# An attention and two feed-forward layers in one kernel: the scores of k in two parts, and the loads of v among those of k

## The chip, the cores and the metric

The kernel runs on one core of one Trainium2 chip. The metric is the device time of one execution in microseconds; the median of three runs is given.

## The reference, cut to what matters

All arrays are float32 at the kernel's inputs except the four weight matrices, which arrive as float64 bits and are converted on the chip. There are 12480 tokens of 128 channels and 49 agents.

```python
def sm(a, b):
    s = scale * (a @ b.transpose(0, 2, 1))
    s = s - s.max(-1, keepdims=True)
    e = np.exp(s)
    return e / (e.sum(-1, keepdims=True) + 1e-09)
agent_v = sm(agents, k) @ v            # 49 x 128, over all 12480 tokens
x = sm(q, agents) @ agent_v            # 12480 x 128
h = x @ w_in                           # 128 -> 2048
x = (h / (1 + np.exp(-h))) @ w_out     # 2048 -> 128
h = x @ w2_in
P = a[0] + a[1] * h + a[2] * h**2 + a[3] * h**3
Q = 1.0 + np.abs(b[0]) * np.abs(h) + np.abs(b[1]) * h**2
out = (P / (Q + 1e-6)) @ w2_out
```

The first softmax runs over all tokens of k, so agent_v needs the whole of k and of v, and every output token needs agent_v.

## The kernel before, in words

The tokens are cut into 25 groups of 512 (the last has 192), and two groups make a block of 1024 tokens (13 blocks, the last of 192 tokens). Every step has a short name, and one function emits its instructions.

**The start.** The loads are issued on SyncE's queue in the order of the string LOADS: a letter k or v is the next block of k or of v (512 KB, the last 96 KB), q is the first block of q, and any other character is one of 16 chunks of the weights (its code less 48: chunks 0 to 3 are w_in, 4 to 7 w_out, 8 to 11 w2_in, 12 to 15 w2_out; 512 KB each). The blocks of k and v go round a ring of 11 buffers, the weight chunks round a ring of 4; a load that finds its buffer in use waits at the head of the queue, and all later loads behind it. For a block b of k, KT transposes it on TensorE, KC copies it out of PSUM on ScalarE, KS makes the scores of the agents, KV keeps them in SBUF and KM (VectorE) takes their maximum. X0 to X2 join the 13 maxima and make the bias; then for each block EX takes exp with its sum on ScalarE, ET transposes on TensorE, EC copies on VectorE, and AV adds eT times v into one PSUM tile. F0 and F1 sum up, F2 divides, F3 and F4 turn the result into agent_v transposed (avT). A weight chunk is converted by C0 (VectorE, three passes), C1 (ScalarE, two), C2 (VectorE, two, the last to read the raw buffer) and C3 (GpSimd); the chunks of w2_in are also split into a high and a low part by C4 (ScalarE, w2h) and C5 (GpSimd, w2l). V0 to V2 multiply w_in by agent_v, which makes the weights w1a and w1b. q's softmax runs a block at a time in the steps QT to QBl.

**The main loop.** For a group g and each p of 8 pairs of 128 hidden channels: M1 (TensorE, h = xt by w1a and w1b), S1 (ScalarE, Silu), M2 (TensorE, into the PSUM tile x2). XS splits x2 into xh and xl. Then M3 (TensorE, three products, w2l and w2h), U, W1 and W2 make P without its last term, AB, N and Q (ScalarE, GpSimd, GpSimd) make the denominator, and L and R (ScalarE, Ln and Sigmoid with a change of table before each batch of four) its reciprocal; G2 joins them and M4 (TensorE) adds into the PSUM tile ot. O1 to O3 write out. M3 of group 0 needs all chunks of w2_in, and AB and U of group 0 need all 16 chunks converted.

**The order.** A planner in the kernel's own code, `scheduled`, writes out the order of all steps at build time: `group_steps` gives each step its engine, an assumed cost, what it comes after, which buffers it takes and ends the use of, and a place; of the steps that are ready on an engine within SLACK, the one with the lowest place goes first. The places are the table PLACE (one number for a step, or one for each p), with `<` and `>` added in the first two and last two groups. READY_Y is the number of halves of y that must be done in a group before its batch of L may begin. PSUM holds three tiles of two banks for h (slots 0 to 2), one bank called x2 and one called ot. On each engine the instructions run in the order written out.

## Time and profile before

| what | before |
|---|---|
| median of 3 runs | 1268.18 us (1267.84 to 1269.21) |
| the profiled execution's own time | 1269.22 us |
| its span, first to last instruction | 1267.4 us |
| TensorE (PE) busy | 1238.8 us, 98% of the span |
| ScalarE (ACT) busy | 1076.2 us, 85% |
| VectorE (DVE) busy | 1002.5 us, 79% |
| GpSimd (POOL) busy | 765.2 us, 60% |

Shares are means over the whole span, and the start, the main loop and the end have different limits. A busy PE is not PE at its peak, as matmuls are pipelined and run at the clock that is granted (1.00 is the full 2.4 GHz, 0.50 is 1.2 GHz). A wait is put down to the releaser that came last.

### The profile page before, as it was taken

To read this page: it belongs to the slowest core of one execution; us is meant where nothing else is said; L and a number is where in the kernel's file an instruction comes from. 1 tells how busy PE (TensorE), PEld (TensorE's weight loads), DVE (VectorE), ACT (ScalarE), POOL (GpSimd) and SP (SyncE) were. 2 spreads that over 40 slices of the span, in tenths; PEclk is the share of its full clock that TensorE was granted. 3 is DMA by queue.
4 is the path that set the end of the run, shared out by engine and by line. 5 is a ranking of instruction groups with operands and counts; after the bars stand their busy time and mean duration, and the time that the engine had idled before them with its cause. 6 is when DMAs were issued, how large, how long until landed. Compare 5 with 4: busy or idle time off the path is not lost.

```text
span 1267.4 us, 12079 instructions
## 1 busy us (share of the span) xinstructions
PE 1238.8 (98%) x4393; PEld 742.1 (59%) x4393; DVE 1002.5 (79%) x960; ACT 1076.2 (85%) x997; POOL 765.2 (60%) x434
## 2 busy tenths in 40 slices
PE   9899899999999999999999999999999999999987
PEld 5656555555556566566566565565555555555654
DVE  4977787878869869869869769769769769768894
ACT  7676888988988988988978978978978978978895
POOL 2247767567656656655755755755755755756873
PEclk9899899999999999999999999999999999999999
DMA  9820000000000000000000000000000000000000
GB/s 336 302 83 1 1 17 9 9 17 9 9 17 9 9 18 9 9 17 9 9 17 9 9 17 9 9 17 9 2 24 8 1 12 9 1 9 8 9 1 20
DMA packets 14675, 34.75 MB, mean 27 GB/s; under 512 B 1575, under 2 KB 5720, under 8 KB 14616
## 3 DMA queue, kind: packets, MB, share of 16 engines
q1 hardware_dynamic: 14616, 33.98, 7.5%
q8 instruction: 35, 0.57, 0.2%
q14 instruction: 24, 0.20, 0.1%
HBM read 27.59 MB, written 6.39 MB: 27 GB/s over the span
## 4 chain that ended last, share of the span: by engine, by line
PE 86%; DVE 6%; ACT 4%; DMA 3%; issue 1%; POOL 0%; SPq 0%; POOLq 0%; ACTq 0%; DVEq 0%
PE x L551 25%; PE ot L635 24%; PE h L537 7%; PE h L574 7%; PE h L538 7%; PE h L576 7%; PE h L575 7%; DVE z L610 2%; DVE z L614 1%; PE h L468 1%; DVE z L585 1%; PE h L451 1%; DMA kv<-in_k_dram 1%; DMA q<-in_q_dram 1%; PE ot L655 1%
## 5 line engine op out<-in xcount | busy, mean ns | idle before, releaser
L598 POOL TENSOR_SCALAR y<-m,bab 128x1024 f32<-128x1024 f32 (+1 forms) x200 | 266.0, 1333 | 410.0 <-ACT m L592 403.1
L606 POOL TENSOR_TENSOR y<-y,m 128x1024 f32<-128x1024 f32 (+1 forms) x200 | 469.1, 2357 | 7.5
L635 PE MATMUL ot<-z,w2o 128*128 128x512 f32 (+1 forms) x800 | 357.4, 587 | 7.5 <-DVE z L626 4.6
L551 PE MATMUL x<-s,wo 128*128 128x512 f32 (+1 forms) x800 | 357.6, 582 | 3.4 <-ACT s L544 3.2
L610 DVE TENSOR_TENSOR z<-z,h 128x1024 f32<-128x1024 f32 (+1 forms) x200 | 237.7, 1191 | 143.7 <-ACT z L583 136.6
L626 DVE SCALAR_TENSOR_TENSOR z<-z,a_sb,y 128x1024 f32<-128x1024 f32 (+1 forms) x200 | 263.0, 1365 | 4.7 <-ACT y L622 4.7
L592 ACT ACTIVATE m<-h 128x1024 f32<-128x1024 f32 (+1 forms) x200 | 197.1, 1000 | 81.1 <-PE h L576 72.7
L614 DVE SCALAR_TENSOR_TENSOR z<-z,a_sb,h 128x1024 f32<-128x1024 f32 (+1 forms) x200 | 249.9, 1251 | 5.0 <-ACT m L592 0.5
L635 PEld LDWEIGHTS ot<-z,w2o 128*128 128x128 f32 x800 | 149.1, 190 | 164.2 <-issue 146.1
L544 ACT ACTIVATE s<-h 128x1024 f32<-128x1024 f32 (+1 forms) x200 | 193.4, 1005 | 59.6 <-PE h L538 58.5
L551 PEld LDWEIGHTS x<-s,wo 128*128 128x128 f32 x800 | 147.3, 190 | 138.8 <-issue 126.9
L574 PE MATMUL h<-xh,w2l 128*128 128x512 f32 (+1 forms) x400 | 190.8, 477 | 1.7 <-DVE z L614 1.2
L619 ACT ACTIVATE y<-y,eps 128x2048 f32<-128x2048 f32 (+1 forms) x100 | 191.4, 1956 | 0.8 <-POOL y L606 0.5
L537 PE MATMUL h<-xt,w1a 128*128 128x512 f32 (+1 forms) x400 | 185.8, 466 | 0.7 <-DVE z L614 0.7
L622 ACT ACTIVATE y<-y 128x2048 f32<-128x2048 f32 (+1 forms) x100 | 184.9, 1878 | 0.3
L576 PE MATMUL h<-xh,w2h 128*128 128x512 f32 (+1 forms) x400 | 155.7, 389 | 0.0
L538 PE MATMUL h<-xt,w1b 128*128 128x512 f32 (+1 forms) x400 | 155.2, 389 | 0.0
L575 PE MATMUL h<-xl,w2h 128*128 128x512 f32 (+1 forms) x400 | 155.0, 387 | 0.0
L585 DVE TENSOR_SCALAR z<-h,a_sb 128x1024 f32<-128x1024 f32 (+1 forms) x100 | 130.9, 1313 | 5.7 <-PE h L576 3.8
L583 ACT ACTIVATE z<-h,a_sb 128x1024 f32<-128x1024 f32 (+1 forms) x100 | 118.3, 1184 | 8.3 <-PE h L576 4.6
L537 PEld LDWEIGHTS h<-xt,w1a 128*128 128x128 f32 x400 | 75.5, 189 | 43.6 <-issue 15.8
L574 PEld LDWEIGHTS h<-xh,w2l 128*128 128x128 f32 x400 | 75.7, 189 | 36.8 <-issue 20.6
(105 smaller groups left out, 849.5 us busy)
## 6 DMA issues: line engine op xcount, KB each, us to landing
q<-in_q_dram SPq DMA_DIRECT2D x12, 512.0 KB, 3.3
out_dram<-ob SPq DMA_DIRECT2D x24, 256.0 KB, 2.0
raw<-in_moe_w_in_dram SPq DMA_DIRECT2D x8, 512.0 KB, 5.4
raw<-in_moe_w_out_dram SPq DMA_DIRECT2D x8, 512.0 KB, 7.5
s<-in_k_dram SPq DMA_DIRECT2D x7, 512.0 KB, 8.4
kv<-in_v_dram SPq DMA_DIRECT2D x7, 512.0 KB, 7.4
kv<-in_k_dram SPq DMA_DIRECT2D x5, 512.0 KB, 10.2
s<-in_v_dram SPq DMA_DIRECT2D x5, 512.0 KB, 8.6
```

What stands on the lines that cost most here:

```text
L537: nc.tensor.matmul(h[:, c, :w], w1a[:, f], xt, start=True, stop=False)
L538: nc.tensor.matmul(h[:, c, :w], w1b[:, f], xt, start=False, stop=True)
L551: nc.tensor.matmul(x2_t[i][:, : cols(i)], wo[:, 2 * p + c, :], s[:, c, : cols(i)], start=(p == 0 and c == 0), stop=(p == NP - 1 and c == 1),)
L574: nc.tensor.matmul(h[:, c, :w], w2l[:, f], xh_t[i], start=True, stop=False)
L575: nc.tensor.matmul(h[:, c, :w], w2h[:, f], xl_t[i], start=False, stop=False)
L576: nc.tensor.matmul(h[:, c, :w], w2h[:, f], xh_t[i], start=False, stop=True)
L598: nc.gpsimd.tensor_scalar(out=y_t[i, p // 2][:, p % 2], in0=m_t[i, p], scalar1=bab[:, 1:2], scalar2=bab[:, 0:1], op0=ALU.mult, op1=ALU.add,)
L606: eng.tensor_mul(out=y, in0=y, in1=m_t.pop((i, p)))
L610: nc.vector.tensor_mul(out=z, in0=z, in1=h)
L614: nc.vector.scalar_tensor_tensor(out=z, in0=z, scalar=a_sb[:, 1:2], in1=h, op0=ALU.add, op1=ALU.mult)
L626: nc.vector.scalar_tensor_tensor(out=z, in0=z, scalar=a_sb[:, 0:1], in1=r, op0=ALU.add, op1=ALU.mult)
L635: nc.tensor.matmul(ot_t[i][:, : cols(i)], w2o[:, 2 * p + c, :], z[:, c, :], start=(p == 0 and c == 0), stop=(p == NP - 1 and c == 1),)
```

## The change

LOADS is another order: blocks of v stand among those of k, q comes late, and the weight chunks are spread otherwise. The blocks of k are taken in two parts, 0 to 6 and 7 to 12 (HALF = 7). Each part has its own maximum, and EX of a block waits for the maximum of its own part alone. The bias of part two is that of part two's own maximum. AV adds part one into the first 128 columns of its PSUM tile and part two into the next 128. X2 of part two also takes the common maximum, and the differences of the two maxima to it; the new step XE takes exp of them. F0 sums each part, weighs the sums by these factors and adds; F2 weighs the two products and adds. The scores of blocks 7 to 12 all go to the PSUM bank ot, where before odd blocks went to x2.

In the planner, S1, AB, U and N of a group now come after all eight of the group before (IN_TURN), and AB of an odd p after that of the p before. SLACK, READY_Y, some costs and all of PLACE have other numbers.

```diff
--- before.py
+++ after.py
@@ -27,7 +27,9 @@
 NX = 1
 NKV = 11
 
-LOADS = "kk0kkkkk1kkkvkk2q4kvvvvvv><vvv56vv37?v;=:98"
+HALF = 7
+
+LOADS = "kkkk2kkkvk4kvk18vvv3kkvvv6vvk0<vvq:?;>5v79="
 
 
 
@@ -42,56 +44,58 @@
     "QBl": ("DVE", 1.24), "C0": ("DVE", 1.06), "C1": ("ACT", 1.06), "C2": ("DVE", 1.22),
     "C3": ("POOL", 1.35), "C4": ("ACT", 0.52), "C5": ("POOL", 1.7), "LD": ("DMA", 1.32),
     "KT": ("PE", 0.88), "KC": ("ACT", 1.0), "KS": ("PE", 0.95), "KV": ("ACT", 0.5),
-    "KM": ("DVE", 0.61), "X0": ("DVE", 0.15), "X1": ("PE", 0.15), "X2": ("DVE", 0.2),
-    "EX": ("ACT", 0.6), "ET": ("PE", 0.45), "EC": ("DVE", 0.61), "AV": ("PE", 1.05),
-    "F0": ("DVE", 0.1), "F1": ("PE", 0.1), "F2": ("DVE", 0.35), "F3": ("PE", 0.25),
+    "KM": ("DVE", 0.61), "X0": ("DVE", 0.15), "X1": ("PE", 0.15), "X2": ("DVE", 0.3),
+    "XE": ("ACT", 0.2), "EX": ("ACT", 0.6), "ET": ("PE", 0.45), "EC": ("DVE", 0.61), "AV": ("PE", 1.05),
+    "F0": ("DVE", 0.35), "F1": ("PE", 0.1), "F2": ("DVE", 0.65), "F3": ("PE", 0.25),
     "F4": ("DVE", 0.25), "V0": ("PE", 0.87), "V1": ("ACT", 0.6), "V2": ("DVE", 0.61),
 }
 PLACE = {
...
 }
-SLACK = {"PE": 0.0, "ACT": 0.0, "DVE": 0.0, "POOL": 7.0}
-READY_Y = 4
+SLACK = {"PE": 0.26, "ACT": 0.0, "DVE": 0.63, "POOL": 12.26}
+READY_Y = 3
 TAIL = {"PE": 0.17, "ACT": 0.125, "DVE": 0.085, "POOL": 0.02, "DMA": 2.0}
 
 BATCH = {
     "QT", "QTc", "QS", "QV", "QX", "QM", "QE", "QN", "QB", "QBc", "QBl", "KT", "KC", "KS", "KV", "KM", "EX", "ET", "EC", "AV",
 }
 PRE = {"LD", "C0", "C1", "C2", "C3", "C4", "C5", "V0", "V1", "V2"}
+
+IN_TURN = {"S1", "AB", "U", "N"}
 
 TELL = {
     "PE": {"PE": -0.17, "ACT": 0.04, "DVE": 0.04}, "ACT": {"PE": 0.055, "DVE": 0.035, "POOL": 0.1, "ACT": 0.03},
     "DVE": {"PE": 0.055, "ACT": 0.095, "POOL": 0.1, "DVE": 0.035},
     "POOL": {"ACT": 0.1, "DVE": 0.1, "PE": 0.06, "POOL": 0.06}, "DMA": {"DMA": -2.0},
 }
-TABLE = {"S1": "silu", "L": "ln", "R": "sigmoid", "QE": "exp", "EX": "exp"}
+TABLE = {"S1": "silu", "L": "ln", "R": "sigmoid", "QE": "exp", "EX": "exp", "XE": "exp"}
 SWITCH = 1.41
 
 PORT = {"N", "Q", "G2", "QN", "C0", "C2", "C3", "C5"}
@@ -105,6 +109,8 @@
     ops = {}
 
     def add(name, g, p, after=(), takes=(), uses=(), at=None, cost=None):
+        if name in IN_TURN and g:
+            after = list(after) + [(name, g - 1, n) for n in range(pairs)]
         place = PLACE.get(name, (0.0,))
         at = g + place[p % len(place)] if at is None else at
         if name not in BATCH and name not in PRE and (name[0] not in "XF" or name == "XS"):
@@ -135,11 +141,11 @@
             add(name, b, 0, after, takes, uses, at=at + PLACE[name][0])
         step("KT", [land["k", b]], [("h", ("kp", b))], [("k", b)])
         step("KC", [("KT", b, 0)], [("kT", ("kT", b))], [("kp", b)])
-        tag = "x2" if b % 2 else "ot"
+        tag = "x2" if b % 2 and b < HALF else "ot"
         step("KS", [("KC", b, 0)], [(tag, ("ks", b))], [("kT", b)])
         step("KV", [("KS", b, 0)], [], [("ks", b)])
         step("KM", [("KS", b, 0)], [], [("ks", b)])
-        step("EX", [("X2", 0, 0), ("KV", b, 0)])
+        step("EX", [("X2", int(b >= HALF), 0), ("KV", b, 0)])
         step("ET", [("EX", b, 0)], [("h", ("ep", b))])
         step("EC", [("ET", b, 0)], [("eT", ("eT", b))], [("ep", b)])
         step(
@@ -148,10 +154,13 @@
         )
     b = 0
     at = -4
-    step("X0", [("KM", n, 0) for n in range(batches)])
-    step("X1", [("X0", 0, 0)], [("ot", ("xp", 0))])
-    step("X2", [("X1", 0, 0)], [], [("xp", 0)])
-    step("F0", [("EX", n, 0) for n in range(batches)])
+    for b in range(2):
+        step("X0", [("KM", n, 0) for n in range(batches) if (n >= HALF) == b])
+        step("X1", [("X0", b, 0)], [("ot", ("xp", b))])
+        step("X2", [("X1", b, 0)] + [("X2", 0, 0)] * b, [], [("xp", b)])
+    b = 0
+    step("XE", [("X2", 1, 0)])
+    step("F0", [("XE", 0, 0)] + [("EX", n, 0) for n in range(batches)])
     step("F1", [("F0", 0, 0)], [("ot", ("fp", 0))])
     step("F2", [("F1", 0, 0), ("AV", batches - 1, 0)], [], [("fp", 0), ("av", 0)])
     step("F3", [("F2", 0, 0)], [("ot", ("fq", 0))])
@@ -193,7 +202,8 @@
             add("U", g, p, [("M3", g, p)] + (conv if g == 0 else []), [("z", z)], [h], cost=u)
             add("W1", g, p, [("U", g, p)], [], [h, z])
             add("W2", g, p, [("W1", g, p)], [], [h, z])
-            add("AB", g, p, [("M3", g, p)] + (conv if g == 0 else []), [("m", m)], [h])
+            before = (conv if g == 0 else []) + [("AB", g, p - 1)] * (p % 2)
+            add("AB", g, p, [("M3", g, p)] + before, [("m", m)], [h])
             add("N", g, p, [("AB", g, p)] + [("N", g, p - 1)] * (p % 2), [("y", y)] if p % 2 == 0 else [], [m, y])
             add("Q", g, p, [("N", g, p)], [], [m, y], cost=("DVE", 1.14) if p in Q_DVE else ("POOL", 2.375))
         for h in range(4):
@@ -829,7 +839,7 @@
     def KS(b):
         kT = kT_t.pop(b)
         m, n = blocks(b)
-        ps = ps_t[b] = (t_x2() if b % 2 else t_ot())[:, : m * n]
+        ps = ps_t[b] = (t_x2() if b % 2 and b < HALF else t_ot())[:, : m * n]
         for h in range(2):
             nc.tensor.matmul(
                 ps[h * LO : (h + 1) * LO, :], agT, kT[:, h, :], start=True, stop=True
@@ -842,23 +852,37 @@
         nc.vector.reduce_max(out=mxs[:, b : b + 1], in_=ps_t[b], axis=AX.X)
 
 
-    mx = pool.tile([P, 4], F32, name="mx", bufs=1)
-
-    def X0(_):
-        nc.vector.reduce_max(out=mx[:, 0:1], in_=mxs, axis=AX.X)
-
-    def X1(_):
-        ps = ps_t["x"] = t_ot()
+
+    mine = pool.tile([P, 2], F32, name="mine", bufs=1)
+    mx = pool.tile([P, 2], F32, name="mx", bufs=1)
+    bias = pool.tile([P, 2], F32, name="bias", bufs=1)
+    top = pool.tile([P, 1], F32, name="top", bufs=1)
+    to_top = pool.tile([P, 2], F32, name="to_top", bufs=1)
+    parts = (slice(0, HALF), slice(HALF, NK))
+
+    def X0(i):
+        nc.vector.reduce_max(out=mine[:, i : i + 1], in_=mxs[:, parts[i]], axis=AX.X)
+
+    def X1(i):
+        ps = ps_t["x", i] = t_ot()
         for h in range(2):
             nc.tensor.matmul(
                 ps[h * LO : (h + 1) * LO, :1], ident[:, (1 - h) * LO : (2 - h) * LO],
-                mx[:, 0:1], start=True, stop=True,
+                mine[:, i : i + 1], start=True, stop=True,
             )
 
-    def X2(_):
-        nc.vector.tensor_max(out=mx[:, 1:2], in0=ps_t["x"][:, :1], in1=mx[:, 0:1])
-        nc.vector.tensor_scalar_mul(out=mx[:, 2:3], in0=mx[:, 1:2], scalar1=-SCALE)
-        nc.scalar.activation(bab, b_sb, AF.Abs)
+    def X2(i):
+        o = slice(i, i + 1)
+        nc.vector.tensor_max(out=mx[:, o], in0=ps_t["x", i][:, :1], in1=mine[:, o])
+        nc.vector.tensor_scalar_mul(out=bias[:, o], in0=mx[:, o], scalar1=-SCALE)
+        if i == 0:
+            nc.scalar.activation(bab, b_sb, AF.Abs)
+        else:
+            nc.vector.tensor_max(out=top, in0=mx[:, 0:1], in1=mx[:, 1:2])
+            nc.vector.tensor_scalar_sub(out=to_top, in0=mx, scalar1=top)
+
+    def XE(_):
+        nc.scalar.activation(to_top, to_top, AF.Exp, scale=SCALE)
 
     avT = pool.tile([P, 2, LO], F32, name="avT", bufs=1)
     nc.gpsimd.memset(avT, 0.0)
@@ -866,7 +890,8 @@
 
     def EX(b):
         nc.scalar.activation(
-            part(b), part(b), AF.Exp, scale=SCALE, bias=mx[:, 2:3], accum_out=sums[:, b : b + 1]
+            part(b), part(b), AF.Exp, scale=SCALE, bias=bias[:, int(b >= HALF) :][:, :1],
+            accum_out=sums[:, b : b + 1],
         )
 
     def ET(b, slot):
@@ -886,22 +911,28 @@
     def AV(b):
         if b == 0:
             ps_t["av"] = t_x2()
-        av, eT = ps_t["av"], eT_t.pop(b)
+        i = int(b >= HALF)
+        av, eT = ps_t["av"][:, i * C :], eT_t.pop(b)
         m, n = blocks(b)
         for j in range(m):
             for h in range(2):
                 nc.tensor.matmul(
                     av[h * LO : (h + 1) * LO, :C], eT[:n, j, h * LO : (h + 1) * LO],
-                    v_t[b][:n, h * m + j, :], start=(b + j == 0),
-                    stop=(b == NK - 1 and j == m - 1),
+                    v_t[b][:n, h * m + j, :], start=(b in (0, HALF) and j == 0),
+                    stop=(b in (HALF - 1, NK - 1) and j == m - 1),
                 )
 
+    total = pool.tile([P, 3], F32, name="total", bufs=1)
+
     def F0(_):
-        nc.vector.reduce_sum(out=mx[:, 3:4], in_=sums, axis=AX.X)
+        for i in range(2):
+            nc.vector.reduce_sum(out=total[:, i : i + 1], in_=sums[:, parts[i]], axis=AX.X)
+        nc.vector.tensor_mul(out=total[:, :2], in0=total[:, :2], in1=to_top)
+        nc.vector.reduce_sum(out=total[:, 2:3], in_=total[:, :2], axis=AX.X)
 
     def F1(_):
         ps_t["f"] = t_ot()
-        nc.tensor.matmul(ps_t["f"][:, :1], fold, mx[:, 3:4], start=True, stop=True)
+        nc.tensor.matmul(ps_t["f"][:, :1], fold, total[:, 2:3], start=True, stop=True)
 
     rs = pool.tile([P, 1], F32, name="rs", bufs=1)
     avs = pool.tile([P, C], F32, name="avs", bufs=1)
@@ -909,7 +940,12 @@
     def F2(_):
         nc.vector.tensor_scalar_add(out=rs, in0=ps_t["f"][:, :1], scalar1=1e-9)
         nc.vector.reciprocal(out=rs, in_=rs)
-        nc.vector.tensor_scalar_mul(out=avs, in0=ps_t["av"][:, :C], scalar1=rs)
+        nc.vector.tensor_scalar_mul(out=to_top, in0=to_top, scalar1=rs)
+        nc.vector.tensor_scalar_mul(out=avs, in0=ps_t["av"][:, :C], scalar1=to_top[:, 0:1])
+        nc.vector.scalar_tensor_tensor(
+            out=avs, in0=ps_t["av"][:, C : 2 * C], scalar=to_top[:, 1:2], in1=avs,
+            op0=ALU.mult, op1=ALU.add,
+        )
 
 
     def F3(_):
@@ -945,7 +981,7 @@
     one = {
         "C0": conv_bits, "C1": conv_parts, "C2": conv_join, "C3": conv_out, "C4": conv_high,
         "C5": conv_low, "LD": LD, "KT": KT, "KC": KC, "KS": KS, "KV": KV, "KM": KM, "X0": X0,
-        "X1": X1, "X2": X2, "EX": EX, "ET": ET, "EC": EC, "AV": AV, "F0": F0, "F1": F1, "F2": F2,
+        "X1": X1, "X2": X2, "XE": XE, "EX": EX, "ET": ET, "EC": EC, "AV": AV, "F0": F0, "F1": F1, "F2": F2,
         "F3": F3, "F4": F4, "V0": V0, "V1": V1, "V2": V2,
     }
     late = None
```

## Rows read from the trace of the kernel before

**Rows 1.** Page, part 1: busy us (share of the span) and instructions.
```profile
PE 1238.8 (98%) x4393; PEld 742.1 (59%) x4393; DVE 1002.5 (79%) x960; ACT 1076.2 (85%) x997; POOL 765.2 (60%) x434
```

**Rows 2.** Windows by stage: length, busy us by engine, clock, DMA share, GB/s.
```profile
0.00:67.70 67.70, 60.47 (x459) 41.12 (x460) 46.54 (x95) 44.48 (x84) 16.35 (x23) 0.92 0.85 307
...
147.00:161.00 14.00, 8.88 (x20) 4.78 (x19) 8.64 (x7) 11.11 (x10) 8.66 (x5) 0.76 0.00 1
161.00:1203.00 1042.00, 1040.65 (x3444) 616.63 (x3445) 837.58 (x734) 909.70 (x787) 654.66 (x352) 1.00 0.03 11
1203.00:1267.40 64.40, 51.24 (x209) 32.30 (x207) 45.29 (x54) 48.17 (x52) 34.26 (x24) 0.96 0.03 10
```

**Rows 3.** Timeline of PE, 59 to 69 us: start, us, what.
```profile
60.17 0.65 PE L893 MATMUL x<-s,eT 48*64 48x128 f32 x8
...
67.71 0.79 PE L537 MATMUL h<-xt,w1a 128*128 128x512 f32 x1
```

**Rows 4.** Timeline of SyncE's queue, waits inside its us.
```profile
33.80 8.84 SPq L694 DMA_DIRECT2D kv<-in_v_dram  x2
...
49.79 6.15 SPq L703 DMA_DIRECT2D raw<-in_moe_w_out_dram  x2
56.04 0.45 SPq L694 DMA_DIRECT2D s<-in_v_dram  x1
```

**Rows 5.** Timeline of DVE, 48 to 61 us.
```profile
48.41 0.16 DVE L900 TENSOR_REDUCE mx<-sums 128x1 f32<-128x13 f32 x1
...
50.08 1.39 DVE L714 TENSOR_SCALAR ex<-raw 128x512 uint32<-128x512 uint32 x1 [0.31 <-DMA raw<-in_moe_w_out_dram]
...
52.06 1.27 DVE L884 COPY eT<-h 128x512 f32<-128x512 f32 x2
...
54.87 0.67 DVE L741 SCALAR_TENSOR_TENSOR sb<-raw,sb 128x512 uint32<-128x512 uint32 x1
...
60.87 0.35 DVE L912 TENSOR_SCALAR avs<-x,rs 128x128 f32<-128x128 f32 x1 [0.72 <-PE x L893]
```

**Rows 6.** Windows of the start, columns as in rows 2.
```profile
2.00:22.00 20.00, 19.13 (x117) 12.86 (x117) 8.58 (x16) 13.22 (x21) 4.82 (x10) 1.00 0.99 381
32.00:42.00 10.00, 7.32 (x48) 5.12 (x44) 9.06 (x21) 9.07 (x25) 1.72 (x2) 0.72 1.02 370
...
37.50:43.50 6.00, 5.97 (x35) 5.32 (x36) 4.94 (x11) 6.00 (x17) 1.27 (x1) 0.52 1.02 353
```

**Rows 7.** Timeline, 0 to 80 us, KM of block 6.
```profile
22.75 0.69 DVE L842 TENSOR_REDUCE mxs<-ot 128x1 f32<-128x512 f32 x1 [1.34 <-PE ot L834]
```

**Rows 8.** Timelines of DVE, POOL and PE, 92 to 112 us.
```profile
96.27 0.69 DVE L565 TENSOR_TENSOR xl<-x,xh 128x512 fp32r<-128x512 f32 x1
...
99.28 1.27 POOL L764 TENSOR_TENSOR w2l<-w,w2h 128x512 fp32r<-128x512 f32 x1 [0.19 <-ACT w2h L760]
...
100.17 0.80 PE L574 MATMUL h<-xh,w2l 128*128 128x512 f32 x1
```

**Rows 9.** Timelines of POOL and ACT, 110 to 178 us.
```profile
132.43 2.39 POOL L606 TENSOR_TENSOR y<-y,m 128x1024 f32<-128x1024 f32 x1
...
133.17 1.28 ACT L619 ACT_TABLE_LOAD   x1
```

**Rows 10.** Timeline of PE, 110 to 178 us; in brackets the idle time before.
```profile
150.22 3.78 PE L635 MATMUL ot<-z,w2o 128*128 128x512 f32 x4 [3.21 <-DVE z L626]
...
160.91 1.98 PE L551 MATMUL x<-s,wo 128*128 128x512 f32 x4 [1.91 <-ACT s L544]
```

**Rows 11.** The chain that ended last, 112 to 180 us: start, us, what.
```profile
154.00 0.43 PE h L537
...
156.35 0.23 PE h L576
```

**Rows 12.** Timeline of PE, 1200 to 1267 us.
```profile
1209.33 0.47 PE L574 MATMUL h<-xh,w2l 128*128 128x512 f32 x1 [0.68 <-DVE z L614]
...
1237.34 3.19 PE L635 MATMUL ot<-z,w2o 128*128 128x512 f32 x4 [2.19 <-ACT ob L661]
```

56 rows, old and new, of the table PLACE are left out of this document.

## Prediction

> **What bounds the kernel now.** I read the page first. PE is busy for 98% of the span [rows 1]. So the time is PE's work plus the places where PE has nothing to do or runs slowly, and the change can only act on those. I then cut the span into stages [rows 2]. From 161 to 1203 us PE is busy for 1040.65 of 1042 us: there is nothing to gain there, only something to lose. The loose time lies in three places. In the start, 0 to 67.7 us, PE is busy for 60.5 us at a mean clock of 0.92, and group 0's first M1 comes at its end. In a hole at 147 to 161 us PE is busy for 8.9 us of 14 at 0.76. In the last 64.4 us it is busy for 51.2.
>
> **The start** ends with a chain that no order can shorten: the last block of v (v12, 192 tokens), its AV product, F2 to F4, V0 to V2, M1. AV(12) begins at 60.17 and M1 at 67.71, so 7.5 us lie behind v12 [rows 3]. v12 itself was not late because the DMA engines were slow. SyncE's queue issues loads in the written order; it stood 8.84 us (two loads, the second for AV(0) to free its buffer), then 6.15 us at w7 and w15, and only then, at 56.04, issued v12, which PE used 4.1 us later [rows 4]. w15 wanted the raw buffer of w5, four weight loads back, and this was free when the second half of w5's conversion on DVE ended, 54.87 + 0.67 = 55.54; w5's first conversion step began at 50.08 [rows 5]. So from a weight chunk's arrival to its buffer's release took 5.5 us.
>
> **The change, part by part.** *The central barrier goes.* Today nothing after the maximum can run until all 13 blocks are scored; around it the clock fell, to a mean of 0.52 at 37.5 to 43.5 us, which is about 2.9 us of PE's work lost [rows 6]. With two parts, EX, ET, EC and AV of blocks 0 to 6 run among the KT and KS of blocks 7 to 12. KM of block 6 ran at 22.75 us in the old order [rows 7], so part one's maximum can stand at about 24 us, and AV(0), five steps of under 1.2 us later, can end near 28. I cost this at nothing in the sum: what it frees on PE and DVE lies ahead of v12's arrival, which ends the start. If v12 came early, it would be worth the 2.9 us.
>
> *The loads.* v12 was load 37, counted from 0, and becomes load 39. Ahead of it, w5 becomes load 38 and wants the buffer of w10, load 34, four weight loads back: the same wait as today. When does w10 land? Loads 0 to 34 are 34 of 524,288 bytes and k12's 98,304, together 17.9 MB. Where the engines were full they moved 381 and 370 GB/s [rows 6]; 375 makes 47.8 us, and from the first bytes at about 2 us this is 49.8. Then 5.5 us to the buffer's release as for w5, 0.5 to v12's issue (55.54 to 56.04), and 4.1 to its use: 59.9 against 60.1 today. Bounds: w10 could be converted without the EC copies that stood between w5's steps for 1.27 us [rows 5], which gives 58.6; or SyncE stands at w11 and w14 as well, whose buffers are those of w0 and w12 (loads 29 and 30), and three conversions queue on DVE between EC copies: about 3 us more, 62.9. What stands behind SyncE's waits are w5, v12 and the three loads after them, and nobody else. A second wait is new: v6 (load 23) takes v0's buffer and waits for AV(0), near 28 us, where its turn is near 24. That is 4 us on a queue that stood 8.84 with the engines at a share of 1.02 all the while [rows 4, 6]; I take it as hidden by the loads already issued; uncovered it would cost those 4 us.
> The Trainium skill's page "DMA: Bandwidth & Descriptors" (Specifications) gives one core about 358 GB/s of HBM; by that w10 would land at 52.1 and v12 be used at 62.2, 2.3 us later than by the rows. The trace's 381 GB/s over 20 us lies above that figure.
>
> *Added small operations.* A second X0 to X2, a maximum and a difference, XE on ACT, three more sums and products in F0, two more operations in F2: about ten instructions on DVE and one on ACT; a reduction of 13 numbers took 0.16 us [rows 5], so 1.6 us on DVE. All but one lie ahead of v12's arrival. Behind it stands one more pass over 128x128, the scalar_tensor_tensor that adds part two; the pass it follows took 0.35 us [rows 5]. +0.35. (If part one's product is also held back by the shared PSUM tile, it is where today's pass is: no more.) KS of blocks 7 to 12 has one PSUM bank instead of two in turn, as part two's accumulator holds the other; six blocks, about 1 us each, covered by the wait for v. Start in sum: -0.2 + 0.35 = about +0.2 us, between -1.5 and +3.
>
> *The weights.* Today the last loads are w11, w13, w10, w9, w8. M3 of group 0 wants w8's split: xl was ready at 96.27 + 0.69 = 96.96, but POOL finished w2l at 100.55 and M3 began right after it, in the row that starts at 100.17 [rows 8]. In the new order w8 is load 15 and w9 and w13 are the last, six loads sooner behind v12 than w8 was. So M3(0) is then held by xl alone: 3.8 us sooner.
>
> *The order of the main loop.* All places, slacks and READY_Y are new, and S1, AB, U and N of a group wait for those of the group before. READY_Y 3 lets group 0's Ln run when three of four halves of y are done. POOL's last Q of group 0 took 2.39 us up to 134.8, and Ln's table load came at 133.17 [rows 9]; Ln need no longer wait for the last two, so up to about 5 us.
>
> These two act on the hole. At 147 us PE had run out of M1 to M3 and stood 3.21 us for the first M4, which waited for G2, R, Ln and POOL; the clock then fell and M4's four matmuls took 3.78 us; and at 160.91 PE stood 1.91 us more for S1, which ACT ran late [rows 10]. The four M1 matmuls after M4 took 0.43 us each, against 0.23 for one at the full clock [rows 11]; half of 3.78 + 4 x 0.43 + 0.4 is 2.95 us lost to the clock. The hole is 3.2 + 2.95 + 1.9 = 8.1 us. An M4(0) that comes 3.3 us sooner closes the first two terms, and 3.8 plus some of 5 us are on offer. The third hangs on ACT's backlog of Ln, Sigmoid and U, which stays: I leave it. Taken: -6.2; bounds 0 (PE also gets to its end of work sooner) and -8.1.
>
> *Middle and end.* The middle holds 1.35 us of idle PE. I take 0 for both. The end has 13 us of idle PE in which the last two groups drain, and a new order can move it either way; bounds -3 and +3, as a single wait there takes up to 2.2 us [rows 12].
>
> **The sum.** The profiled execution took 1269.2 us, 1267.4 of it span, and stands 1.0 above the median of 1268.2. 1269.2 + 0.2 - 6.2 = 1263.2; against the median 1262.2.
>
> **The rivals.** *The hole stays, or the start eats what it gives* (no change that can be measured, within 0.2%, which is 2.5 us and about the least that this kernel's runs can tell). For it: S1, Ln, Sigmoid and U share ACT, and if M1 to M3 also run ahead faster, PE waits for M4(0) as before. Then the time is 1268.2 + 0.2, and with v12 late by 3 us and the hole closed 1265.2. Against it: the 3.3 us needed are fewer than what w8 alone gives. Chance 0.19.
> *The new order leaves PE waiting in every group* (slower). The in-turn rule lets no S1, AB or U pass those of the group before. PE stood 0.68 us for DVE at 1209.33 where two groups' work met [rows 12]. The same once in each of the 22 groups of the middle is 15 us: 1262.2 + 15 = 1277. It decides from 0.4 us a group (8.7 us over 22): above that the kernel is slower by over 0.2%. Against it: ACT and DVE are busy for 910 and 838 of 1042 us there [rows 2], so they have room of 13% and 20%. One hole like that at 147, opened elsewhere, would cost 8 us and leave the time at 1270. Chance 0.19.
> *The start truly shortens* (faster by more): v12's buffer wait is short, the freed PE time counts, and the end gains 3: 1262.2 - 1.7 - 1.9 - 3 = 1255.6. Chance 0.12.
> *The change does not do what it says:* v6's wait for AV(0) drains the queue, and the weights behind it shift by its 4 us; the maximum in two parts gives nothing. With the hole closed this is 1266.2; it is within the no-change chance.
>
> **How the numbers follow.** The forecast (hole closed, start as it is) has 0.50, the shorter start 0.12: faster by over 0.2% 0.62. No change 0.19, slower 0.19. The likeliest is 1262.2, with its own range 1258 to 1266. The range to hold 8 in 10 reaches down to 1254.5, just past the shorter start, and up past no change and one new hole (1270) to 1273; what lies above is over half of the slower rival, what lies below a part of the shorter start.
>
> **What would show it.** Right: AV's first product before 30 us; no stretch at half clock near 40 us; SyncE still standing ahead of v12, and the first M1 between 66 and 71 us; M3's first before 98; no wait of PE for M4 over 1 us near 147 and the clock at 1.00 there; PE's idle time in the middle under 3 us. Wrong: a first M1 past 71, the hole at its old size or moved, new waits in the middle with the clock falling after them, or an end longer by several us.

## The result: slower by about 1.1%

| what | before | after |
|---|---|---|
| median of 3 runs | 1268.18 us | 1281.96 us (1280.72 to 1284.45) |
| ratio, 95% interval | | 1.0115 (1.0101 to 1.0128) |
| span of the profiled execution | 1267.4 us | 1280.1 us |
| first M1 | 67.71 us | 80.55 us |
| from the first M1 to the end of the span | 1199.69 us | 1199.55 us |

The forecast was 1262.2 us, with a range of 1254.5 to 1273. The time lies above it. The last two rows of the table say where to look: the first M1 comes 12.84 us later, and everything behind it takes as long as before. So the whole loss is in the start, and the 6.2 us that the hole was to give did not come either.

### The profile after

Windows by stage of the changed kernel, columns as in [rows 2]. The cuts follow its own first M1 and its own hole.

```profile
0.00:67.70 67.70, 54.87 (x439) 38.06 (x441) 45.13 (x89) 42.27 (x81) 17.37 (x24) 0.90 0.83 306
67.70:80.55 12.85, 8.75 (x28) 4.24 (x25) 8.38 (x17) 4.22 (x8) 4.08 (x3) 0.60 0.01 3
...
157.00:175.00 18.00, 14.70 (x51) 9.40 (x52) 17.34 (x14) 17.44 (x15) 8.68 (x6) 1.00 0.00 1
175.00:1215.70 1040.70, 1036.86 (x3431) 614.17 (x3429) 841.66 (x730) 913.22 (x786) 670.61 (x352) 1.00 0.03 10
1215.70:1280.10 64.40, 51.24 (x192) 33.27 (x192) 44.83 (x51) 45.98 (x51) 35.74 (x25) 0.91 0.03 10
37.50:43.50 6.00, 4.74 (x48) 3.00 (x48) 5.31 (x10) 3.92 (x6) 2.39 (x2) 1.00 1.05 356
48.00:60.00 12.00, 8.26 (x45) 5.39 (x44) 9.15 (x22) 7.15 (x17) 3.84 (x3) 0.50 0.54 178
```

Against [rows 2, 6]: PE is busy for 54.87 us of the first 67.7 where it was busy for 60.47, and then 8.75 of 12.85 at a clock of 0.60. The half clock at 37.5 to 43.5 us is gone (1.00 for 0.52), as the first barrier was to do; but there is a new one at 48 to 60 us, where PE is busy for 8.26 of 12 us and the clock is at 0.50, the lower level of 1.2 GHz. The middle has 3.84 us of idle PE for 1.35.

Timeline of PE in the changed kernel, the start.

```profile
28.20 1.97 PE L919 MATMUL x<-kv,eT 128*64 128x128 f32 x32
...
43.67 0.45 PE L829 MATMUL h<-ident,s 48*128 48x48 f32 x4
46.22 1.96 PE L844 MATMUL ot<-w2o,agT 128*64 128x512 f32 x4 [2.11 <-DVE mxs L852]
49.58 0.58 PE L844 MATMUL ot<-w2o,agT 128*64 128x96 f32 x4 [1.40 <-DVE mxs L852]
...
68.86 0.65 PE L919 MATMUL x<-s,eT 48*64 48x128 f32 x8 [0.86 <-DMA s<-in_v_dram]
...
73.33 0.69 PE L953 MATMUL ot<-fold,avs 128*128 128x64 f32 x2 [0.82 <-DVE avs L945]
74.52 6.60 PE L962 MATMUL h<-wi,avT 128*128 128x512 f32 x8 [0.51 <-DVE avT L957]
80.55 0.79 PE L547 MATMUL h<-xt,w1a 128*128 128x512 f32 x1
```

AV's first product is at 28.20. Then part two: block 12's KT is at 43.67, and KS of blocks 11 and 12 (46.22 and 49.58) wait 2.11 and 1.40 us for VectorE to take the maximum out of the one PSUM bank that is left. At the end AV(12) is at 68.86, where it was at 60.17 [rows 3], and the eight V0 products, with the first M1 behind them at 80.55, take 6.0 us.

Timeline of DVE: the second maximum, and the end of the start.

```profile
43.73 1.50 DVE L729 TENSOR_SCALAR ma<-raw 128x512 uint32<-128x512 uint32 x1
45.15 0.41 DVE L733 TENSOR_SCALAR ec<-ex 128x512 f32<-128x512 uint32 x1
...
51.88 0.15 DVE L876 TENSOR_TENSOR mx<-ot,mine 128x1 f32<-128x1 f32 x1
...
67.09 0.55 DVE L499 TENSOR_REDUCE qmx<-h 128x8 f32<-128x392 f32 x1
...
70.19 1.08 DVE L512 TENSOR_TENSOR e<-e,qsm 128x392 f32<-128x392 f32 x1
71.20 0.15 DVE L941 TENSOR_SCALAR rs<-ot 128x1 f32<-128x1 f32 x1
...
72.53 0.35 DVE L944 TENSOR_SCALAR avs<-x,to_top 128x128 f32<-128x128 f32 x1
```

The second maximum is at 51.88; the single one of before was at 36.12. Timeline of PE in the kernel before, block 12's KT:

```profile
31.21 0.45 PE L819 MATMUL h<-ident,s 48*128 48x48 f32 x4
```

So of the 15.76 us, 12.46 stand already at block 12's KT (43.67 for 31.21); from there to the maximum it takes 8.21 us in place of 4.91. At the end the row at 71.20 (F2) stands behind q's softmax (67.09 to 71.27), so avs is made at 72.53 in place of 60.87 [rows 5].

SyncE's queue, the rows that answer to [rows 4].

```profile
33.46 0.33 SPq L704 DMA_DIRECT2D s<-in_k_dram  x1
...
40.16 0.33 SPq L452 DMA_DIRECT2D q<-in_q_dram  x1
...
57.28 7.29 SPq L713 DMA_DIRECT2D raw<-in_moe_w_out_dram  x2
64.62 0.49 SPq L704 DMA_DIRECT2D s<-in_v_dram  x1
```

The row at 33.46 is k12's load. It landed some 10 us later, when block 12's KT began (43.67). q's first load comes only at 40.16, and v12 is issued at 64.62, behind 7.29 us at w14 and w5, where it was issued at 56.04.

### The profile page after: what moved, and what is told of

Read it like the earlier page. It is cut to its first block, busy times and chain, and to the rows that moved or that the text cites. A ratio compares the mean times of both kernels' runs of the same rounds, so it can differ in the third digit from the quotient of the medians.

```text
span 1280.1 us, 12113 instructions
## 1 busy us (share of the span) xinstructions
PE 1241.2 (97%) x4397; PEld 744.7 (58%) x4397; DVE 1018.9 (80%) x970; ACT 1081.5 (84%) x1000; POOL 781.5 (61%) x434
## 4 chain that ended last, share of the span: by engine, by line
PE 83%; DVE 8%; ACT 5%; DMA 2%; issue 1%; SPq 0%; POOL 0%; POOLq 0%; ACTq 0%; DVEq 0%
PE x L561 23%; PE ot L645 23%; PE h L547 7%; PE h L548 6%; PE h L584 6%; PE h L586 6%; PE h L585 6%; DVE z L620 2%; DVE z L624 2%; DVE z L636 1%; PE h L478 1%; DVE z L595 1%; ACT m L602 1%; DMA kv<-in_v_dram 1%; DMA b_sb<-in_moe_b_dram 1%
## 5 line engine op out<-in xcount | busy, mean ns | idle before, releaser
L608 POOL TENSOR_SCALAR y<-m,bab 128x1024 f32<-128x1024 f32 (+1 forms) x200 | 272.1, 1362 | 396.2 <-ACT m L602 391.2
L616 POOL TENSOR_TENSOR y<-y,m 128x1024 f32<-128x1024 f32 (+1 forms) x200 | 479.9, 2410 | 10.3
L645 PE MATMUL ot<-z,w2o 128*128 128x512 f32 (+1 forms) x800 | 351.6, 585 | 4.9 <-DVE z L636 3.6
L547 PE MATMUL h<-xt,w1a 128*128 128x512 f32 (+1 forms) x400 | 197.0, 494 | 0.7 <-ACT s L554 0.5
L584 PE MATMUL h<-xh,w2l 128*128 128x512 f32 (+1 forms) x400 | 184.4, 461 | 8.7 <-ACT s L554 2.6
L593 ACT ACTIVATE z<-h,a_sb 128x1024 f32<-128x1024 f32 (+1 forms) x100 | 115.6, 1181 | 8.9 <-PE ot L645 7.3
L547 PEld LDWEIGHTS h<-xt,w1a 128*128 128x128 f32 x400 | 75.7, 189 | 43.5 <-issue 19.4
```

What stands on the lines that cost most here:

```text
L547: nc.tensor.matmul(h[:, c, :w], w1a[:, f], xt, start=True, stop=False)
L584: nc.tensor.matmul(h[:, c, :w], w2l[:, f], xh_t[i], start=True, stop=False)
L608: nc.gpsimd.tensor_scalar(out=y_t[i, p // 2][:, p % 2], in0=m_t[i, p], scalar1=bab[:, 1:2], scalar2=bab[:, 0:1], op0=ALU.mult, op1=ALU.add,)
L616: eng.tensor_mul(out=y, in0=y, in1=m_t.pop((i, p)))
L645: nc.tensor.matmul(ot_t[i][:, : cols(i)], w2o[:, 2 * p + c, :], z[:, c, :], start=(p == 0 and c == 0), stop=(p == NP - 1 and c == 1),)
```

## The experiments

Three theories stood at first. **A**: the second part's maximum is late, because k12 is load 28 (it was load 18) and part two's scores go through one PSUM bank with weight conversions between them on VectorE. **B**, the prediction's own chain: v12's load stands behind w5's buffer. **C**: the order on VectorE at the end, F2 behind q's softmax. Later came **D** (the half clock), **S** (two parts cost this in themselves) and **R** (q's chain alone). Each run is told by its first M1, as the times of single runs differ by some us. The stage itself differs from run to run too: the second maximum is at 51.88 in the changed kernel and at 50.60 to 51.82 in e1, e2, e3 and e11, whose edits do not touch what is ahead of it. A shift of about 1 us in one run shows nothing. The kernel before, run beside them, took 1265.5 to 1267.7 us.

| run | second maximum | avs | first M1 | time |
|---|---|---|---|---|
| before | 36.12 (the only one) | 60.87 | 67.71 | 1268.18 |
| changed | 51.88 | 72.53 | 80.55 | 1281.96 |
| e1, v12 early | 51.40 | 72.07 | 80.09 | 1281.45 |
| e2, F2 first | 51.53 | 69.20 | 81.81 | 1284.96 |
| e3, both | 50.60 | 67.57 | 78.60 | 1281.8 |
| e4, conversions late | 49.85 | 75.87 | 88.27 | 1290.66 |
| e5, filler | 53.69 | 77.24 | 88.31 | 1291.39 |
| e6, two parts, other order | 48.50 | 63.45 | 69.36 | 1273.55 |
| e7, one part, other order | 34.66 | 59.92 | 66.06 | 1272.27 |
| e8, e6 with q late | 47.68 | 67.89 | 76.32 | 1278.91 |
| e9, e6 with v12 late | 47.72 | 63.86 | 72.15 | 1273.93 |
| e10, e6 with k12 late | 52.15 | 67.11 | 74.21 | 1277.46 |
| e11, filler at the end | 51.82 | 72.48 | 81.08 | 1282.03 |
| e12, cut at block 10 | 44.67 | 58.34 | 64.88 | 1271.05 |

### e1: v12's load early

The order that the planner wrote is changed by hand: one step moves ahead of another, here v12's load ahead of q's and of five weight chunks.

```diff
+    ahead("LD", 39, "LD", 33)
```

> Three theories of why the first M1 begins at 80.55 us and not at 67.71. A: the second part's maximum stands only at 52 us (its last block of k is load 28, and its blocks pass one PSUM bank with weight conversions between them on DVE), so that its six blocks of EX, ET, EC and AV end late. B (the prediction's step): the last block of v, v12, is loaded late behind w5's buffer. C: on DVE the steps that end the start (F2) stand behind q's softmax and conversions. This run issues v12's load six loads earlier and changes nothing else. By B the first M1 comes 6 to 8 us sooner and the time is 1274 to 1276. By A and C AV(12) gains at most the 0.9 us that it waited for the load, F2 nothing, and the time stays at 1281 to 1282.

M1 came 0.46 us sooner, and the second maximum, which v12 does not touch, 0.48: v12 gave nothing. The prediction had taken v12 for the thing that ends the start; with v12 there in time, AV(12) follows AV(11) at once and the start ends where it did. B falls as the cause.

### e2: F2 ahead of q's softmax

```diff
+    for name, n in (("AV", 11), ("AV", 12), ("F2", 0), ("F3", 0), ("F4", 0), ("V0", 0)):
+        ahead(name, n, "QM", 0)
```

> The last two AV, F2, F3, F4 and the first V0 are written ahead of q's softmax (QM to QB) of block 0; the loads stay. By C F2 begins right behind AV(12), 2 to 3 us sooner, and the first M1 1.5 to 3 us sooner (q's own chain then ends last): 1279 to 1280.5. By B and A it gains under 1 us, as AV(12) stays where it is and q's chain is only pushed back.

avs came 3.33 us sooner (69.20 for 72.53) and M1 1.26 us later. q's softmax, pushed back, now ends last: QBl is at 77.51, and V0's other products and M1 stand behind it on PE. C alone does not make the loss.

### e3: both

```diff
+    ahead("LD", 39, "LD", 33)
+    for name, n in (("AV", 11), ("AV", 12), ("F2", 0), ("F3", 0), ("F4", 0), ("V0", 0)):
+        ahead(name, n, "QM", 0)
```

> v12's load six loads earlier and F2 ahead of q's softmax, together. By B the first M1 is at 70 to 72 and the time 1272 to 1274. By C about 3.5 us sooner than the changed kernel, 1278.5. By A the two together give 2 to 4 us, and at least 9 of the 12.8 us stay, as AV(11) ends at 66 to 68 us still.

avs came 4.96 us sooner (67.57), M1 only 1.95. Timeline of PE in e3:

```profile
69.30 1.34 PE L961 MATMUL h<-wi,avT 128*128 128x512 f32 x2 [0.51 <-DVE avT L956]
73.31 1.11 PE L521 MATMUL h<-ident,e 128*128 128x128 f32 x4 [2.67 <-DVE e L512]
...
77.21 1.95 PE L961 MATMUL h<-wi,avT 128*128 128x512 f32 x4 [1.08 <-DVE xt L532]
```

The V0 product of 69.30 could have been followed by the rest and by M1; but PE's next instruction is q's last transpose, which waits 2.67 us for q's softmax; V0 goes on at 74.22, and its last four rows wait another 1.08 us, to 77.21, for xt, q's last step. So two chains end the start: agent_v's and q's. Each hides what the other gains.

### e4: conversions behind the second maximum

```diff
+    for n in (6, 3):
+        for name in ("C3", "C2", "C1", "C0"):
+            behind(name, n, "X2", 1)
+    for n in (35, 34):
+        behind("LD", n, "C2", 6)
```

(on top of e3; 6 and 3 are the chunks w6 and w3, 35 and 34 the loads that take their buffers)

> As e3_both, and the conversions of w3 and w6, which stand among the maxima of blocks 8 to 12 on DVE, moved behind the second part's bias; the loads of w10 and w15, which need their buffers, move with them. By A the second maximum comes at 46 to 48 us in place of 52, and the first M1 3 to 5 us sooner than in e3_both, unless the conversions moved then stand before EC. By B and C nothing is gained over e3_both, and the two conversions now late can cost 1 to 2 us.

Against e3 the second maximum moved by 0.75 us only, and M1 went 9.67 us back: the conversions now stood between the maximum and EX on ScalarE, and EX(7) began at 58.38 (53.15 in the changed kernel). With them out of the way, block 12's KT waited 1.65 us for its load and KS(12) still 1.40 for the one bank. So taking these two chunks away does not bring the maximum to the 46 to 48 us that A expected, and where they go instead costs more than they took.

### e5: filler matmuls, to hold the clock

About 90 matmuls on ones, which nothing reads, go into PE's waits.

```diff
+    for at_, n, slot in (
+        (("KT", 12), 16, 2), (("KS", 11), 12, 2), (("KS", 12), 6, 2), (("X1", 1), 2, 2),
+        (("EC", 7), 6, 1), (("F1", 0), 10, 0), (("AV", 11), 8, 2), (("AV", 12), 16, 2),
+        (("QB", 0), 8, 2), (("F3", 0), 6, 2),
+    ):
+        order.insert(at(*at_) + 1, ("fill", n, 0, slot))
```

> The changed kernel with about 90 more 128x128 matmuls on ones put into TensorE's waits of the start (24 to 75 us), so that the clock does not fall to its half there; they write to a PSUM slot of h and nothing reads them. Theory D (the loss is the half clock at 48 to 60 and 72 to 81 us): the first M1 comes 3 to 4.5 us sooner, near 76 to 77.5, and the time falls to 1277 to 1279. Theory A (the end of the start follows three chains on VectorE and ScalarE, of part two's scores, of v12 and of q's softmax, and TensorE only waits for them): the clock rises but the first M1 moves by under 1.5 us, and only in its last stretch from V0 to M1 (6.0 us against 4.8 at the better clock).

M1 went to 88.31. Timeline of PE in e5:

```profile
69.51 4.10 PE L1010 MATMUL h<-ones 128*128 128x128 f32 x20 [3.21 <-DVE e L500]
...
84.95 3.67 PE L961 MATMUL h<-wi,avT 128*128 128x512 f32 x8
```

The fillers of 69.51 waited 3.21 us for a PSUM slot that q's scores still held, and AV(11) stood behind them: the run says nothing on D as a whole. But from V0 to M1 it took 3.36 us (84.95 to 88.31) where the changed kernel took 6.03 at half the clock. So 2.7 us of that stretch are the clock, against the full one. Against the kernel before, whose V0 to M1 took 4.81 us at a clock of 0.65, it is 1.22 us.

### e6 and e7: the start's order written anew, with two parts and with one

The start up to the first M1 is given as a list, chosen by the planner's own costs; the planner, with 1.4 us for a load in place of 1.32, goes on from there, so that the loop's order can shift too. The operations are unchanged. In e6 only LOADS and the list differ from the changed kernel, in e7 from the kernel before.

```diff
-LOADS = "kkkk2kkkvk4kvk18vvv3kkvvv6vvk0<vvq:?;>5v79="
+LOADS = "kkkk2k4kkk8k1kvv3vkkq6<vv0vk:vvvvvv;v5?>7=9"
...
-    for name, g, p, slot in scheduled(NG, NP, REST / GW):
+    for name, g, p, slot in scheduled(NG, NP, REST / GW, start):
```

> The same two parts with the same operations, one PSUM bank for part two's scores, and the main loop by the same rules; only the order of the start up to the first M1, the loads included, is written out anew: v12 is load 36 in place of 39, q load 20 in place of 33, k12 load 27 in place of 28, and the weight chunks go between and behind. Theory A (the order: the three chains that end the start all came late, and each held M1 when another was moved): the first M1 comes at 68 to 73 and the time is 1267 to 1273, near that of before. Theory S (the two parts themselves cost it: a second maximum behind one bank, with TensorE waiting at each score for VectorE's maximum): the second maximum stays at 50 to 52, M1 past 76, the time past 1275.

> The kernel before, with one maximum, and its start's order and loads written out anew in the same way (v12 load 35 in place of 37, q load 13 in place of 16). Theory A (an order, not the number of parts, sets the start): the first M1 is within 3 us of that of the two parts written out anew, at 66 to 70, and the time is 1266 to 1271. Theory S (two parts cost what the change lost): M1 at 66 to 70 here and 8 or more later with two parts.

e6: 1273.55 us, ratio to before 1.0042 (1.0028 to 1.0056); the first M1 at 69.36, 11.19 us sooner than in the changed kernel. So nearly all of the loss was an order, as A has it, not the two parts (S); the time lies just above the 1273 that A allowed. But A's first piece, the late maximum, is the smaller one: it moved by 3.38 us (51.88 to 48.50). And k12's load had no part in that: block 12's KT is at 45.78, 2.11 us later than in the changed kernel, and from there to the maximum it takes 2.72 us in place of 8.21. What shortened are the steps behind the load, the handing on of the one bank and what stood between the maxima on VectorE; the run does not part these. From the maximum to avs it took 14.95 us in place of 20.65, and from avs to M1 5.91 in place of 8.02. Timelines of DVE and then of PE in e6:

```profile
48.50 0.16 DVE L903 TENSOR_TENSOR mx<-ot,mine 128x1 f32<-128x1 f32 x1 [0.47 <-PE ot L896]
...
55.47 0.55 DVE L526 TENSOR_REDUCE qmx<-h 128x8 f32<-128x392 f32 x1
...
62.25 0.57 DVE L539 TENSOR_TENSOR e<-e,qsm 128x392 f32<-128x392 f32 x1
...
63.45 0.35 DVE L971 TENSOR_SCALAR avs<-x,to_top 128x128 f32<-128x128 f32 x1
```

```profile
45.78 0.45 PE L856 MATMUL h<-ident,kv 48*128 48x48 f32 x4
...
61.23 1.68 PE L946 MATMUL x<-s,eT 128*64 128x128 f32 x24 [0.15 <-DVE eT L936]
...
65.58 2.81 PE L989 MATMUL h<-wi,avT 128*128 128x512 f32 x6 [0.90 <-DVE avT L984]
```

q's maximum is at 55.47 and its softmax ends with the row at 62.25, just ahead of F2, whose first row is at 62.73; AV(12) waits 0.15 us, not for its load. The chains now end together.

e7: 1272.27 us, ratio 1.0033 (1.0022 to 1.0043), slower than before although its first M1 is 1.65 us sooner, and above the 1271 that A allowed. Some of the 1.65 is order alone, as half of its V0 products come behind the first M1 (at 68.38 and 71.32); avs is 0.95 sooner. Against e6, one part is 3.53 us ahead at avs and 3.30 at M1; whether that is the price of a second part or of two different orders is not shown. The first M3 is at 100.17 in e7, as in the kernel before: what M1 won was gone by then.

### e8, e9, e10: one thing put back in e6

In e8 and e10 the planner also chose the three slots of h anew, where e6's list names them.

```diff
 e8, q's first load at place 33, its chain behind part two's last blocks
+LOADS = "kkkk2k4kkk8k1kvv3vkk6<vv0vk:vvvvvqv;v5?>7=9"
 e9, v12's load at place 39, behind w5, w15 and w14
+LOADS = "kkkk2k4kkk8k1kvv3vkkq6<vv0vk:vvvvvv;5?>v7=9"
 e10, k12's load at place 30
+LOADS = "kkkk2k4kkk8k1kvv3vkkq6<vv0v:vvkvvvv;v5?>7=9"
```

> The two parts in the order of e6 with one thing put back: q's first load at place 33, as in the changed kernel, in place of 20, and q's softmax behind the last blocks of part two, as there. Theory A (three chains end the start, each of them by itself able to hold it): q's last step comes after v12's product again, and the first M1 is at 74 to 79 against 69.36 in e6. Theory R (q's chain alone was what held the start, and the other two have room): M1 goes all the way back, to 79 to 81. If q's place does not matter, M1 stays within 1 us of 69.4.

> The order of e6 with v12's load put back from place 36 to 39, behind w5, w15 and w14, of which each waits for a raw buffer; nothing else is moved. Theory A: v12 is used at 65 to 70 in place of 61.9, and the first M1 comes at 73 to 78 against 69.36. Theory R (only q's chain counted): M1 moves by under 1 us, as it did when v12 alone came sooner in e1.

> The order of e6 with k12's load put back from place 27 to 30, behind w10 and two blocks of v, and k12's steps behind that; nothing else is moved. Three loads are 4.2 us at 375 GB/s. Theory A: the second maximum moves from 48.50 to 52 to 53 and the first M1 with it, to 72 to 74, as every product of part two waits for that maximum. Theory R: the second maximum moves but the first M1 stays within 1.5 us of 69.4, as v12 and q end later than the products of part two.

**e10** did what A said, or nearly so (M1 at 74.21 for 72 to 74). Timelines of PE and then of DVE in e10:

```profile
49.35 0.66 PE L855 MATMUL h<-ident,kv 48*128 48x48 f32 x4 [3.51 <-DMA kv<-in_k_dram]
```

```profile
52.15 0.16 DVE L902 TENSOR_TENSOR mx<-ot,mine 128x1 f32<-128x1 f32 x1 [0.56 <-PE ot L895]
```

Block 12's KT waits 3.51 us for its load; the maximum moved by 3.65 us, avs by 3.66, M1 by 4.85. k12's place goes through to avs in full. The other 1.2 us are the clock from V0 to M1: 4.98 us at 0.66, in e6 3.78 at 1.00.

**e8** put M1 back by 6.96 us, as A said (74 to 79) and not all the way as R said; 1.2 us of it lie between V0 and M1, as in e10. It moved more than was meant. SyncE's queue in e8:

```profile
42.73 16.72 SPq L478 DMA_DIRECT2D q<-in_q_dram  x2
...
60.45 0.42 SPq L730 DMA_DIRECT2D s<-in_v_dram  x1
```

q's first and second load stand in one row of 16.72 us, as the second waits for QT to free the buffer of the first; v12, behind it, is issued at 60.45 in place of 46.43, and AV(12) waited 1.45 us for it. So a late q holds the start twice, by its own softmax and by the loads queued behind its second block; the run does not part the two.

**e9** missed what A expected (73 to 78), and R too (under 1 us). v12 was issued 12 us later (58.69), but avs moved by 0.41 us only, or by 1.19 counted from the second maximum, which was at 47.72 for 48.50. Timeline of PE in e9:

```profile
63.17 0.65 PE L946 MATMUL x<-s,eT 48*64 48x128 f32 x8 [1.62 <-DMA s<-in_v_dram]
...
65.99 6.72 PE L989 MATMUL h<-wi,avT 128*128 128x512 f32 x8 [0.90 <-DVE avT L984]
```

AV(12) waited 1.62 us, and then the eight V0 products ran at half the clock, 6.72 us for eight. M1's 2.79 us are thus 0.4 of delay and 2.4 of clock. v12 had room in e6; of A's three chains k12's is shown to hold the start, q's only together with the loads behind it, and v12's is not.

### e11: fillers in the last stretch alone

```diff
+    for at_, n, slot in ((("AV", 12), 16, 2), (("QB", 0), 8, 2), (("F3", 0), 8, 2)):
+        order.insert(at(*at_) + 1, ("fill", n, 0, slot))
```

(on the changed kernel)

> The changed kernel with 32 matmuls of 128x128 on ones in the waits of the start's last stretch alone: 16 behind v12's product, 8 behind q's last transpose, 8 behind F3, into a slot of h whose last reader is done by then. In e5 the same stretch ran at the clock 1.00 and V0 to the first M1 took 3.4 us, where the changed kernel takes 6.0 (74.52 to 80.55). Theory D, for the share that is left to it: V0 to M1 falls to 3.4 to 4 us, M1 comes 1.5 to 2.6 us sooner, near 78 to 79, and the time is 1279 to 1280.5. If the clock does not rise by these few matmuls, nothing moves by more than 0.5 us.

The time is that of the changed kernel: 1282.03 us, ratio to before 1.0124 (1.0106 to 1.0142). Timeline of PE in e11:

```profile
69.44 3.84 PE L1006 MATMUL h<-ones 128*128 128x128 f32 x32
...
75.34 0.33 PE L952 MATMUL ot<-fold,avs 128*128 128x64 f32 x2
...
77.72 3.67 PE L961 MATMUL h<-wi,avT 128*128 128x512 f32 x8
```

The clock did rise to 1.00, and V0 to M1 fell to 3.36 us. But the fillers (3.84 us in the first row, and two more lots) stood in PE's queue ahead of q's transpose, F3 and V0: F3 began at 75.34 in place of 73.33, V0 at 77.72 in place of 74.52. What the clock gave, 2.7 us, the fillers took. D has a share in the loss, from V0 to M1 1.22 us against the kernel before, but not one to be had in this way.

### e12: the parts cut at block 10

```diff
-HALF = 7
+HALF = 10
-LOADS = "kkkk2kkkvk4kvk18vvv3kkvvv6vvk0<vvq:?;>5v79="
+LOADS = "2kkkk4kkkkk<kk6qk:vvvkvvv0=vvv53v1>vvv8;7?9"
```

(and other places in PLACE, SLACK and READY_Y; by this string q is load 15 and v12 load 37)

> The two parts cut at block 10 in place of 7 (ten blocks and three), with other loads (k12 at place 21, q at 16, v12 at 35) and other places for the planner; all operations as in the changed kernel. Theory A: the chains of k12, q and v12 are as early as in the kernel before or nearly so, and the first M1 comes at 68 to 72; the time is 1266 to 1273. Theory S (two parts cost 3 us or more at any cut: e6 had its first M1 3.3 us behind one part in an order written the same way): M1 is at 69 to 72 too, but not before 67.7, so that two parts at no cut beat one. If the cut at 10 frees the start of both barriers, M1 comes before 66 and the time is under 1265.

The first M1 came at 64.88, the earliest of all runs and 2.83 us ahead of the kernel before and 1.18 ahead of one part in e7: S falls at this cut. The time is 1271.05 us all the same, ratio 1.0027 (1.0015 to 1.0040). The first M3 is at 99.81, only 0.36 us sooner than before [rows 8]. From there to the end of the span it is 1170.1 us; before it was 1167.2. Windows of e12:

```profile
165.00:1205.50 1040.50, 1036.32 (x3429) 613.68 (x3427) 852.21 (x730) 912.84 (x785) 670.30 (x351) 1.00 0.03 10
```

PE is idle for 4.18 us of this middle, as in the changed kernel (3.84) and in e6 (3.88 of 1031 us), which share its rules for the loop (e12 not all its places); the kernel before and e7 have 1.35 and 1.36.

## Why the prediction was wrong

**The step that failed: "v12's arrival, which ends the start".** The prediction took the chain behind v12 for the only one that can end the start, and costed the two parts "at nothing", since what part one frees lies ahead of v12. That v12's own time was also mis-sized (59.9 forecast, 68.86 measured, as SyncE stood 7.29 us at w14 and w5, having stood at w15 and w11 too) does not matter much: e1 took that wait away, and the start ended where it had. What the prediction did not count is what the new LOADS string does to the other two inputs of the start. k12 went from place 18 to 28 and q from 16 to 33. Part two has a maximum of its own, and all of its EX, ET, EC and AV wait for it; it came at 51.88, 15.8 us behind the old single one: 12.46 up to block 12's KT, and 3.30 in the steps behind it. From the maximum to avs it then took 20.65 us for 24.75. The part that was freed early, part one, is not the part that ends last. e10 shows the price of a load's place, three places of k12 being 3.65 us at the maximum and 3.66 at avs; e6, with block 12's KT no earlier, shows that another order of the same operations gives back 11.19 of the 12.84 us.

By places the 12.84 us are 11.66 up to avs and 1.18 from avs to M1. e3 took 4.96 off the first. Of these 1.28 stand at the second maximum, which its edit does not touch; 3.68 are v12's place and F2's behind q's softmax, taken together, and they come to M1 only when q's chain is early too (e6). Between e3 and e6 avs moves by another 4.12 us. Of this 2.10 is the earlier maximum; what the rest is was not parted.

**One PSUM bank, "covered by the wait for v",** was wrong in the same way: KS(11) and KS(12) waited 2.11 and 1.40 us on the path to the second maximum. On banks the Trainium skill's page "Perfetto Trace Analysis" (Matmul Optimizations) asks that all eight be put to use; here all eight have owners, and the change leaves part two's scores one bank of two, as the other holds the products of AV from 28.20 on. That page's point agrees with the two waits; a second bank for part two was not tried.

**The clock.** I had counted the end of the half clock near 40 us as a gain without use, and that was right. I had not seen the new ones: 48 to 60 us at 0.50, behind PE's wait of 2.11 us ahead of 46.22, and V0 to M1 at half the clock, worth 2.7 us against the full clock by e5 and e11, and 1.22 against the kernel before. What the first of them cost is not shown.

**The hole, -6.2 us: wrong.** From M1 to the first M3 it took 31.05 us for 32.46, 1.4 us less and not 3.8. w8 no longer held it (w2l was done at 107.65), but xl itself was ready 31.29 us after M1 for 29.25, so the 3.8 us shrank. GpSimd's last Q of group 0, the eighth, ended 66.6 us after M1 for 67.1: of the "up to 5 us" half a microsecond was there. PE, GpSimd and ScalarE after the change:

```profile
111.60 0.47 PE L584 MATMUL h<-xh,w2l 128*128 128x512 f32 x1
...
157.62 0.47 PE L584 MATMUL h<-xh,w2l 128*128 128x512 f32 x1 [1.80 <-DVE e L500]
...
163.78 3.70 PE L645 MATMUL ot<-z,w2o 128*128 128x512 f32 x8 [2.62 <-DVE z L636]
```

```profile
139.78 2.40 POOL L616 TENSOR_TENSOR y<-y,m 128x1024 f32<-128x1024 f32 x1
...
144.78 2.40 POOL L616 TENSOR_TENSOR y<-y,m 128x1024 f32<-128x1024 f32 x1
```

```profile
142.37 1.02 ACT L602 ACTIVATE m<-h 128x1024 f32<-128x1024 f32 x1 [0.42 <-PE h L586]
...
145.94 1.28 ACT L629 ACT_TABLE_LOAD   x1
```

The eighth Q is the row at 144.78; with the seventh, at 139.78, three of the four halves were done at 142.18. Ln's table load comes at 145.94, as in the written order it stands behind group 0's last AB (142.37), a U, an S1 and a copy for q: 65.39 us after M1, where it was 65.46 after M1 [rows 9]. In the kernel before, too, it had stood behind ScalarE's own work and not behind the last Q, which ended later, at 134.82:

```profile
131.22 1.93 ACT L544 ACTIVATE s<-h 128x1024 f32<-128x1024 f32 x2
133.17 1.28 ACT L619 ACT_TABLE_LOAD   x1
```

So the "up to 5 us" rested on a wait that the rows do not show. READY_Y was no lever here: written out with 4 in place of 3, the changed order differs in ten places, all from group 23 on. M4 then comes 83.2 us after M1 for 82.5, so the forecast that M4(0) comes 3.3 us sooner failed. The hole did shrink all the same. PE waits 1.80 and 2.62 us, 4.4 in place of 8.1 with the clock's share, and the clock held at 1.00 in 157 to 175; that PE had more other work in hand is the likely reason, and not shown. The middle, taken at 0, gives 2.5 of this back (3.84 us idle for 1.35). In the last 64.4 us PE is busy for 51.24 as before, at a clock of 0.91 for 0.96, which is up to 51.24 x 0.05 = 2.6 us more. The sum, -3.7 + 2.5 + 2.6 = +1.4, stands against -0.14 measured from M1 to the end; closer than that the account does not come.

**The rivals.** "The hole stays, or the start eats what it gives" came nearest in kind, with too small a start. "The new order leaves PE waiting in every group" did not come: the middle lost 2.5 us, not 15. The bounds of the start, -1.5 to +3, were bounds of v12's chain alone, and 12.84 lay outside them.

Right were: AV's first product before 30 us, no half clock near 40, SyncE still standing ahead of v12. Wrong: M1 at 66 to 71, the first M3 before 98 (it was at 111.60), no wait over 1 us before M4, PE's idle time in the middle under 3 us (3.84).

Open stays how much of e8's 6.96 us is q's softmax and how much the loads behind its second block, what in e6 took 5.5 us out of the way from block 12's KT to the maximum, whether a second bank for part two would help, and where e7 and e12 lose 3.8 and 2.9 us behind their first M3, beyond the middle's 2.8 in e12. No version here beats the kernel before.
